# First MoE, last two token blocks: the up products in Strassen's form, with weight sums made in blocks 0 and 1

## The chip, the core and the metric

The kernel runs on one core of a Trainium2 chip. The metric is the device time of one execution in microseconds. The engines are named as in the profile: PE is TensorE's matmul (PEld its weight load), DVE is VectorE, ACT is ScalarE, POOL is GpSimd, SP is SyncE, which here issues the DMAs. PSUM is the memory of eight banks that PE writes to, SBUF the working memory.

## What is computed

Three stages follow one another, all in float32:

```python
# attention, B, H, S, D = 4, 8, 576, 64: causal softmax beside a linear memory
local = softmax(mask(q @ k.T / sqrt(D))) @ v
mem   = (phi(q) @ M_prev) / (phi(q) @ z_prev + 1e-6)
x = (g * mem + (1 - g) * local)            # -> (2304, 512)
# first MoE, d_ff = 2048
h = x @ w_in
y = (h * sigmoid(h)) @ w_out
# second MoE, d_ff = 1536
a = y @ w_gate
out = (a * sigmoid(a) * (y @ w_val)) @ w_out2
```

## The kernel before

A product of two float32 matrices is made from three matmuls: every operand is split into a rounded high part and the rest (hi and lo), and hi.hi, lo.hi and hi.lo are added up in PSUM. A matmul takes 128 x 128 weights and up to 512 columns. ACT makes hi by a cast, DVE or POOL makes lo by a subtraction.

The tokens of the first MoE stand in six blocks: two of batch 0 (256 and 320 tokens) and four of 432 tokens, named t0 to t3. d_ff is cut in 16 tiles j of 128, four tiles to a slice. A *segment* is one block with one slice: four h groups (`s1`, tile j of the up side: 3 x 4 = 12 matmuls into a bank of the pool `ps_m`), then four y groups (512 outputs in four parts e, 12 matmuls each). After an h group comes silu: tanh on ACT (th), a combination on DVE (th again), a cast on ACT (gh), the rest on POOL (gl). `segs` lists the segments in order: blocks of batch 0, then t0 with its four slices, t1 with its four, and then t2 and t3 together, slice by slice. The last 64 groups are those of t2 and t3, called the tail here.

Attention runs beside this: `units` are its steps (batch, pair of heads), cut into slots; a list of goals (`gds`, `gam`) says by which share of the first MoE's work a slot is due. A unit ends with U, the sum of its two parts in PSUM, which `put_x` splits into x (hi on ACT, lo on DVE). x of t2 and t3 is complete with the last unit only.

A third stream is the preparation of the second MoE's weights, `prep_w2`: load a raw tile (`load64`, after a small copy on POOL from the newest gl but one), decode it (L731 on ACT, L732 and L733 on DVE), make sums for Strassen's form on POOL (S), split the parts (cast wo on ACT, subtraction wo on POOL) and store them (`post`, `flush`) to DRAM. The scratch wo has `pw` = 3 buffers. A step of it is taken for 0.55 of the groups from group 50 on; when attention's slots are all placed, `open_w2` closes attention's pools, opens those of the second MoE, takes 0.6 steps a group, and also makes the second MoE's first inputs (`y_prep(0)`: casts of 768 columns on ACT and subtractions of 768 columns on DVE).

The program is written down in this order and then reordered by a scheduler within every engine; `high_priority` lets a part stand earlier. On the chip each engine takes its instructions in the order that came out, and waits on semaphores.

Of the kernel before, what the change touches and what calls it, by code (L numbers as in the profile page):

```python
# [17 lines left out]
P = 128  # L18
# [32 lines left out]
    gds=[0.75, 0.3, 1.25, 0.15, 0.3, 0.5, 1.5, 1.5],  # L51
# [4 lines left out]
    rate=0.55,  # L56
    late=0.6,
    ring=16,
    y0=36,
# [34 lines left out]
def kernel(  # L94
# [251 lines left out]
    def unit(u):  # L346
# [247 lines left out]
        def AV():  # L594
# [33 lines left out]
            for sup, U in Us.items():  # L628
                put_x(b, p, sup, U, E)

# [79 lines left out]
    def load64(w, j, part, after=None):  # L710

        raw = cur["raw"].tile([P, 512, 2], I32, tag="raw8", name="raw8", bufs=CFG["raw8"])
# [12 lines left out]
    def decode(raw, t=None):  # L725
        hi, lo = raw[:, :, 1], raw[:, :, 0]
        u = hi.bitcast(F32)
        if t is None:
            t = cur["raw"].tile([P, 512], F32, tag="raw", name="raw", bufs=CFG["raw"])
# [11 lines left out]
    def raw_w1(*key):  # L741
        if key in seen:
            return None
        if key[0] == 0:
            return load64(w1_in, key[1], 0)
        raw = cur["raw"].tile([P, 512, 2], I32, tag="raw8", name="raw8", bufs=CFG["raw8"])
# [9 lines left out]
    def split_w1(t, key):  # L756
        if key in seen:
            w = wp.tile([P, 2, 512], F32, tag="w", name="w")
            nc.sync.dma_start(out=w, in_=seen[key])
            return r_(w[:, 0]), r_(w[:, 1])  # L760
# [3 lines left out]
        return r_(w[:, 0]), r_(w[:, 1])  # L764

# [49 lines left out]
    for blks in [(0,), (1,), tuple(range(2, NB1))]:  # L815
        for s in [order[-1][1]] + [x for x in range(NSL) if x != order[-1][1]]:
            order += [(("t", i), s) for i in blks]
    segs = []
    for n, (key, s) in enumerate(order):
# [3 lines left out]
            last_use=n + 1 < len(order) and order[n + 1][1] != s,  # L823
        ))

    yps = {}

    def new_yp(key):
# [9 lines left out]
        return t[:, x0:x0 + KD * n].rearrange("p (k n) -> p k n", k=KD)  # L838

    def moe1():  # L840
# [12 lines left out]
        def s1(n, ji):  # L853
# [5 lines left out]
            if ji == 0 and sg["last_use"]:  # L859
                nk = SLICES[segs[n + 1]["s"]]  # L860
                prep1.add([(0, c) for c in nk])
                fresh[0] += len(nk)
            wh, wl = prep1.need((0, j))
# [10 lines left out]
            th = mt.tile([P, TM], F32, tag="th", name="th", bufs=CFG["th"])  # L874
            gh = mg.tile([P, TM], F32R, tag="gh", name="gh")
            gl = mg.tile([P, TM], F32R, tag="gl", name="gl")
            nc.scalar.activation(out=th[:, :nt], in_=ps[:, :nt], func=ACTF.Tanh, scale=0.5 / WS)  # L877
            nc.vector.scalar_tensor_tensor(th[:, :nt], th[:, :nt], 1.0, ps[:, :nt], ALU.add, ALU.mult)  # L878
            cp(CFG["gh" if n >= CFG["n0"] else "gh0"], gh[:, :nt], th[:, :nt])
            tt(CFG["gl" if n >= CFG["n0"] else "gl0"]).tensor_sub(gl[:, :nt], th[:, :nt], f(gh[:, :nt]))  # L880
            gs[n][j] = (gh, gl)
            gate.append(gl[:, 0:1])
# [9 lines left out]
        turn = [0]  # L892

        def bank(name):

            if "g" not in ph2:
                return ps_m.tile([P, 512], F32, tag="m", name=name)
            turn[0] += 1
            i = turn[0] % 7
            if i < 3:  # L900
                return ps_m.tile([P, 512], F32, tag="m", name=name)
            return sum_bank("bd"[i % 2], name)

        LA = CFG["la"]
        for n, sg in enumerate(segs):
# [9 lines left out]
            if n + 1 == len(segs):  # L915
                stream(-1)
            if n + 1 < len(segs) and LA:
                yield from get_x(n + 1)
                for ji in range(LA):
                    yield from s1(n + 1, ji)  # L920
            for e in range(KD):
                ps = bank("y")
                m, last = 0, 3 * len(SLICES[s]) - 1
                for wi, gi in ((0, 0), (1, 0), (0, 1)):
                    for ji, j in enumerate(SLICES[s]):
                        w, g = prep1.need((1, s, e))[wi], gs[n][j][gi]
                        c = slice(P * ji, P * ji + P)
                        nc.tensor.matmul(ps[:, :nt], w[:, c], g[:, :nt], start=(m == 0), stop=(m == last))  # L928
                        m += 1
                if sg["first"]:  # L930
                    nc.scalar.mul(yp[:, e, :nt], ps[:, :nt], 0.5 / WS**2)
                else:
                    nc.vector.scalar_tensor_tensor(
                        yp[:, e, :nt], ps[:, :nt], 0.5 / WS**2, yp[:, e, :nt], ALU.mult, ALU.add
                    )
                if sg["last"]:
                    nc.sync.dma_start(
                        out=yd[P * e:P * e + P, t0:t0 + nt], in_=yp[:, e, :nt]
                    )
                if sg["last_use"]:  # L940
# [4 lines left out]
                    prep1.add([(1, segs[n + 1]["s"], e)])  # L945
# [3 lines left out]


# [19 lines left out]
    def prep_w2():  # L970
        todo = [(j, part) for j in range(F2) for part in range(2)] + [(j, 2) for j in range(F2)]
        raws, post = [], []
# [5 lines left out]

        def flush():
            for d, t in post:  # L980
                nc.sync.dma_start(out=d, in_=t)
            post.clear()
# [9 lines left out]
        def halves(src, n, *dst):  # L992
            w = cur["pw"].tile([P, 4, 256], F32, tag="o", name="wo", bufs=CFG["pw"])
            hi, lo = hl(w, n)
            cp(CFG["whi2"], hi, src)
            tt(CFG["wlo2"]).tensor_sub(lo, src, f(hi))
            if len(dst) == 1:
                post.append((dst[0], w[:, 0:2 * n]))
            else:
                for x, d in enumerate(dst):  # L1000
                    post.append((d, w[:, 2 * x:2 * x + 2]))

# [5 lines left out]
        e = tt(CFG["sS"])  # L1008
        fetch(2)
        for j in range(F2):  # L1010
# [4 lines left out]
            S = cur["pw"].tile([P, 4, 256], F32, tag="S", name="S2", bufs=1)  # L1015
            e.tensor_add(S[:, 0], c[:, 0], c[:, 1])
# [7 lines left out]
            yield  # L1024
            halves(S[:, 2:4], 2, wd2[j][2])
            halves(c[:, 1:2], 1, wd2[j][3])
            yield paused()
        for q in range(NJ2):
# [12 lines left out]
            S = cur["pw"].tile([P, 4, 256], F32, tag="S", name="S2", bufs=1)  # L1041
            e.tensor_sub(S[:, 0], a[:, 1], a[:, 0])
# [6 lines left out]
            yield  # L1049
            halves(S[:, 0:2], 2, to("T1"), to("T2"))  # L1050
# [10 lines left out]
    def y_prep(i):  # L1061
# [9 lines left out]
        def put(nm, src):  # L1071
            y = ph2["yq"].tile([P, 2, 2, HT], F32, tag="y" + nm, name="y" + nm, bufs=1)
# [22 lines left out]
    def open_w2():  # L1095
        yield from drain()
# [3 lines left out]
        ph2["yq"] = ctx.enter_context(tc.tile_pool(name="yq", bufs=1, side="right"))  # L1100
        ph2["yst"] = ctx.enter_context(tc.tile_pool(name="yst", bufs=1, side="right"))
        ph2["xp"] = ExitStack()
        cur["raw"] = ph2["xp"].enter_context(tc.tile_pool(name="rawp2", bufs=1, side="right"))
        cur["pw"] = ph2["xp"].enter_context(tc.tile_pool(name="pw2", bufs=1, side="right"))
        n, y = 0, y_prep(0)
        while left() > 0:
            n += 1
            if int(n * CFG["late"]) > int((n - 1) * CFG["late"]):
                next(ph2["prep"], None)
            if left() <= CFG["y0"] and n % 4 == 1:  # L1110
                next(y, None)
            yield
        for _ in y:
            pass
        for _ in ph2["prep"]:
            pass

    def drain():

        ph2["hold"] = True  # L1120
        for x in ph2["prep"]:
            yield
            if x == "empty":
                break
            yield
        del ph2["hold"]

    def left():

        return sum(2 * NW for _ in segs) - ph2["n"]  # L1130
# [3 lines left out]
    def open_2():  # L1134
        ph2["xp"].close()
# [265 lines left out]
    if True:  # L1401
# [7 lines left out]

        def turn_of(rate):  # L1410
            return int((n_g + 1) * rate) > int(n_g * rate)

        goals, cost, prevc = [], 0, 0
        for sg in segs:
# [4 lines left out]
            prevc = seg_cost(sg)  # L1419
        cost, n_goal = 0, len(goals)  # L1420
        for kind, val in items:
            if kind == "need":
                while slot < val:
# [4 lines left out]
                    slot += 1  # L1428
            else:
# [12 lines left out]
                if slot < NSLOT:  # L1442
                    if "prep" in ph2 and n_g >= CFG["n_prep"] and turn_of(CFG["rate"]):
                        next(ph2["prep"], None)
                else:
                    if "late" not in ph2:
                        ph2["late"] = open_w2()
                    next(ph2["late"], None)
                n_g += 1
                ph2["n"] = n_g  # L1450
# [50 lines left out]
```

## Time and profile before

| | |
|---|---|
| median of 3 runs | 1061.36 us (1060.56 to 1063.29) |
| the profiled execution | 1062.63 us, span 1060.5 us |
| mean granted TensorE clock | 0.992 |
| PE busy | 1035.6 us, 98% of the span |
| DVE, ACT, POOL busy | 637.0, 539.6, 394.6 us |
| end of attention's last U on PE | 501.27 us |
| last matmul of the first MoE | 656.95 us |

The span is measured from the first to the last instruction; the rest of the time lies around it. A busy share is an average over stages. A wait is put down to the engine that released it last.

### The profile page before, as it was taken

How to read it: one execution, taken by the hardware profiler on the slowest of the kernel's cores; microseconds unless marked ns; L12 is line 12 of the kernel's file. 1: busy time of each engine (PE TensorE's matmuls, PEld its weight loads, DVE VectorE, ACT ScalarE, POOL GpSimd, SP SyncE). 2: the span in 40 equal slices, each digit the busy share in tenths (PEclk: the TensorE clock that was granted, in tenths of full speed). 3: DMA queues.
4: the chain of work that ended last, by engine and by line, in shares of the span. 5: the costliest groups of instructions: out<-in, count | busy, mean ns of one | idle time of the engine just before them, and what ended most of it. 6: DMA issues, size and time to landing. Idle time of an engine off the chain costs nothing.

```text
span 1060.5 us, 18824 instructions
## 1 busy us (share of the span) xinstructions
PE 1035.6 (98%) x6622; PEld 954.9 (90%) x6622; DVE 637.0 (60%) x1521; ACT 539.6 (51%) x1259; POOL 394.6 (37%) x461
## 2 busy tenths in 40 slices
PE   7799999999999999999999999999999999999998
PEld 5677988888888899888889999999999999999998
DVE  6796767876555644764254333566845669356573
ACT  6684877866656655664454331333613336133351
POOL 4784654678646556661578751000000000000000
PEclk9899999999999999999999999999999999999999
DMA  8995866468978569852478976777977778877784
GB/s 204 317 301 154 255 225 194 120 231 271 307 248 269 174 226 342 255 191 81 159 244 317 321 250 223 251 256 249 340 261 265 248 250 286 256 265 246 251 287 145
DMA packets 168670, 258.16 MB, mean 243 GB/s; under 512 B 76800, under 2 KB 113152, under 8 KB 168576
## 3 DMA queue, kind: packets, MB, share of 16 engines
q1 hardware_dynamic: 167488, 256.70, 73.1%
q8 instruction: 53, 0.87, 0.3%
q10 hardware_dynamic: 1088, 0.26, 0.1%
q14 instruction: 41, 0.34, 0.1%
HBM read 197.67 MB, written 59.24 MB: 242 GB/s over the span
## 4 chain that ended last, share of the span: by engine, by line
PE 78%; DMA 6%; DVE 4%; POOL 4%; ACT 4%; issue 3%; SPq 1%; POOLq 0%; DVEq 0%; ACTq 0%
PE y L928 15%; PE h L870 13%; PE oac L1205 11%; PE gb L1205 11%; PE po L1312 9%; PE pb L1312 4%; PE gd L1205 4%; PE U L619 3%; PE pst L367 3%; PE pss L434 3%; DMA raw<-in_moe_w_gate_dram 2%; DMA raw<-in_moe_w_val_dram 2%; DVE raw L733 1%; PE pss L509 1%; POOL gl L880 1%
## 5 line engine op out<-in xcount | busy, mean ns | idle before, releaser
L870 PE MATMUL h<-x,w 128*128 128x432 f32 (+2 forms) x1152 | 228.3, 348 | 5.9 <-ACT w L214 3.3
L870 PEld LDWEIGHTS h<-x,w 128*128 128x128 f32 x1152 | 197.8, 191 | 18.3 <-ACT w L214 3.5
L928 PE MATMUL y<-gh,w 128*128 128x432 f32 (+2 forms) x768 | 166.2, 348 | 4.2 <-ACT gh L214 2.3
L928 PEld LDWEIGHTS y<-gh,w 128*128 128x128 f32 x768 | 132.0, 190 | 15.3 <-issue 3.8
L880 POOL TENSOR_TENSOR gl<-th,gh 128x432 fp32r<-128x432 f32 (+2 forms) x96 | 104.7, 1093 | 81.7 <-ACT gh L214 64.9
L1205 PE MATMUL gb<-yT,w 128*128 128x384 f32 x648 | 124.8, 336 | 0.0
L1205 PEld LDWEIGHTS gb<-yT,w 128*128 128x128 f32 x648 | 113.1, 188 | 0.0
L878 DVE SCALAR_TENSOR_TENSOR th<-th,h 128x432 f32<-128x432 f32 (+2 forms) x96 | 52.6, 550 | 79.0 <-ACT th L877 78.9
L523 POOL TENSOR_TENSOR s<-s,r 128x128 f32<-128x128 f32 (+4 forms) x96 | 68.4, 739 | 73.4 <-DVE r L540 20.5
L1312 PE MATMUL po<-w,ph 128*128 128x256 f32 x516 | 93.8, 283 | 0.0
L928 PE MATMUL y<-gl,w 128*128 128x432 f32 (+2 forms) x384 | 88.4, 343 | 0.0
L490 ACT ACTIVATE s<-s,mn 128x128 f32<-128x128 f32 (+3 forms) x128 | 71.0, 557 | 21.4 <-DVE mn L486 19.9
L1205 PE MATMUL oac<-yB,w 128*128 128x384 f32 x432 | 81.3, 336 | 0.0
L1312 PEld LDWEIGHTS po<-w,ph 128*128 128x128 f32 x516 | 81.2, 191 | 0.0
L1277 ACT CAST ph<-r 128x384 fp32r<-128x384 f32 x108 | 51.1, 512 | 55.9 <-DVE r L1231 35.6
L1205 PEld LDWEIGHTS oac<-yB,w 128*128 128x128 f32 x432 | 75.4, 188 | 0.0
L732 DVE TENSOR_SCALAR raw<-raw 128x512 int32<-128x512 int32 x68 | 38.3, 564 | 58.1 <-ACT raw L731 57.8
L214 ACT CAST gh<-th 128x432 fp32r<-128x432 f32 (+2 forms) x96 | 49.0, 513 | 47.0 <-DVE th L878 33.8
L1312 PE MATMUL po<-w,pl 128*128 128x256 f32 x258 | 73.0, 283 | 0.0
L731 ACT ACTIVATE raw<-raw 128x512 f32<-128x512 f32 x68 | 45.6, 671 | 50.0 <-DMA raw<-in_moe_w_gate_dram 19.9
L928 PEld LDWEIGHTS y<-gl,w 128*128 128x128 f32 x384 | 67.6, 190 | 2.9 <-issue 0.5
L1278 DVE TENSOR_TENSOR pl<-r,ph 128x384 fp32r<-128x384 f32 x108 | 55.8, 553 | 17.8 <-ACT ph L1277 17.1
(161 smaller groups left out, 1993.2 us busy)
## 6 DMA issues: line engine op xcount, KB each, us to landing
w<-wg SPq DMA_DIRECT2D x108, 512.0 KB, 4.7
w<-wd SPq DMA_DIRECT2D x80, 512.0 KB, 5.8
wg<-wo SPq DMA_DIRECT2D x36, 512.0 KB, 3.7
w<-woT SPq DMA_DIRECT2D x36, 512.0 KB, 4.7
wd<-w SPq DMA_DIRECT2D x32, 512.0 KB, 4.2
raw<-in_moe_w_out_dram SPq DMA_DIRECT2D x28, 512.0 KB, 5.7
w<-woB SPq DMA_DIRECT2D x27, 512.0 KB, 4.3
w<-wg SPq DMA_DIRECT2D x36, 256.0 KB, 4.8
```

The lines of the kernel that those rows point to most:

```text
L214: nc.scalar.copy(out, in_)
L490: nc.scalar.activation(out=a, in_=a, func=ACTF.Exp, scale=-1.0, bias=mn, accum_out=o["sm", sup][:, col:col + 1])
L523: nc.gpsimd.tensor_mul(a, a, r.to_broadcast([P, w]))
L731: nc.scalar.activation(out=t, in_=u, func=ACTF.Prelu, scale=2.0**-111, alpha=-(2.0**32))
L870: nc.tensor.matmul(ps[:, :nt], w[:, kk, :], x[:, kk, :nt], start=(m == 0), stop=(m == 3 * KD - 1))
L878: nc.vector.scalar_tensor_tensor(th[:, :nt], th[:, :nt], 1.0, ps[:, :nt], ALU.add, ALU.mult)
L880: tt(CFG["gl" if n >= CFG["n0"] else "gl0"]).tensor_sub(gl[:, :nt], th[:, :nt], f(gh[:, :nt]))
L928: nc.tensor.matmul(ps[:, :nt], w[:, c], g[:, :nt], start=(m == 0), stop=(m == last))
L1205: nc.tensor.matmul(dst, w[wi][:, P * kk:P * kk + P], y[ny][:, yi, kk], start=(start and m == 0), stop=(stop and m == 5), skip_group_check= ...
L1277: nc.scalar.copy(ph, src)
L1278: nc.vector.tensor_sub(pl, src, f(ph))
L1312: nc.tensor.matmul(dst, a[:, c], x, start=(begin and m == 0 and own_bank), stop=(end and m == 2), skip_group_check=True,)
```

## The change

The up side of t2 and t3 is no longer made by tile and block. For each of eight pairs of tiles (ja, jc), the 2 x 2 product (two halves of d_model, K0 and K1; two blocks) is made by seven products instead of eight, each of 6 matmuls of 432 columns: `TP` names the weight sides, `TX` the token sides. The weight sums S1 to S4 are made in `combine`, for half of the pairs in t0's segments and for half in t1's, from the weights that lie in SBUF there, and stored to DRAM. The token sums T1 to T4 are made in `first_x` (T1, in the place of x's K0 half of t3) and `tail_x`. The products of a pair go into the banks ha, hb, hc, hd; ACT copies ha into hb and hc into he, DVE adds into hd and he, and four silus follow (`out_of`). The y groups of a slice stand among the products of the next one (`plan`). Preparation starts at group 40 with rates by group, is paused at group 112, and in the tail waits 14 groups and then goes on at 0.45; `y_prep(0)` comes after it.

```diff
-    gds=[0.75, 0.3, 1.25, 0.15, 0.3, 0.5, 1.5, 1.5],
+    gds=[0.75, 0.3, 1.25, 0.15, 1.8],
-    rate=0.55,
-    late=0.6,
+    rate=((40, 0.4), (50, 0.6), (64, 0.75), (96, 0.65)),
+    hold=112,
+    late=0.45,
+    late0=14,
+    urgent=300,
...
-    for blks in [(0,), (1,), tuple(range(2, NB1))]:
+    for blks in [(0,), (1,)]:
...
+    def combine(ja, jc):
+        flush()
+        t = cur["pw"].tile([P, 4, 256], F32, tag="o", name="wo", bufs=CFG["pw"])
+        a, c = (t.rearrange("p a b -> p (a b)")[:, 512 * x:512 * x + 512] for x in range(2))
+        for t, j in ((a, ja), (c, jc)):
+            hi, lo = kept_w[j]
+            nc.vector.tensor_add(t, f(hi), f(lo))
+        S = cur["pw"].tile([P, 4, 256], F32, tag="o", name="wo", bufs=CFG["pw"])
+        nc.vector.tensor_add(S[:, 0], c[:, 0:256], c[:, 256:512])
+        nc.vector.tensor_sub(S[:, 1], S[:, 0], a[:, 0:256])
+        nc.vector.tensor_sub(S[:, 2], a[:, 0:256], c[:, 0:256])
+        nc.vector.tensor_sub(S[:, 3], a[:, 256:512], S[:, 1])
+        for x in range(2):
+            d = seen["S", ja, x] = dram.tile([P, 4, 256], F32, name=f"wsum{ja}_{x}")
+            halves(S[:, 2 * x:2 * x + 2], 2, d)
...
+    TP = ("A11", "S1", "S2", "A12", "S3", "S4", "A22")
+    TX = ("B11", "T1", "T2", "B21", "T3", "B22", "T4")
...
+            if n == 0:
+                ys_ = [("z", e) for e in range(KD)]
+                plan = "p y y p y p p y p p p"
+            else:
+                plan = "p p y p p y p p y p y" if ys_ else "p p p p p p p"
...
+            if p == 0:
+                o["a"] = ph2["ta"].tile([P, 512], F32, tag="a", name="ha")[:, :TB]
+                product(o["a"], it, True)
+                if n > 0:
+                    o["b"] = seeded("b", n)
+                    with urgent():
+                        nc.scalar.copy(o["b"], o["a"])
+            elif p == 1:
...
+                c = sum_bank("d", "hc")[:, :TB]
+                product(c, it, True)
+                o["e"] = ph2["tt"].tile([P, TB], F32, tag="e", name="he", bufs=2)
+                with urgent():
+                    nc.scalar.copy(o["e"], c)
+            elif p == 2:
+                product(o["b"], it, False)
+                o["d"] = seeded("d", n)
+                with urgent():
+                    nc.vector.tensor_add(o["d"], o["b"], o["e"])
+            elif p == 3:
+                product(o["a"], it, False)
+                out_of(n, 0, 0, o["a"])
+            elif p == 4:
+                product(o["b"], it, False)
+                with urgent():
+                    nc.vector.tensor_add(o["e"], o["b"], o["e"])
+                out_of(n, 1, 1, o["e"])
+            elif p == 5:
+                product(o["d"], it, False)
+                out_of(n, 0, 1, o["d"])
+            else:
+                product(o["b"], it, False)
+                out_of(n, 1, 0, o["b"])
...
+    def tail_x():
+        x0, x1 = (xs["t", 2 + h] for h in range(NH))
...
+        whole(a, x1, K0)
+        whole(c, x0, K0)
+        nc.vector.tensor_sub(b, whole(d, x1, K1), a)
+        tx = [ph2["tt"].tile([P, 2, 2, TB], F32R, name="x" + nm) for nm in ("T2", "T3", "T4")]
+        split_x("T2", b, tx[0][:, 0], tx[0][:, 1])
+        nc.vector.tensor_sub(a, b, c)
+        split_x("T3", a, tx[1][:, 0], tx[1][:, 1])
+        nc.vector.tensor_sub(d, whole(d, x0, K1), b)
+        split_x("T4", d, tx[2][:, 0], tx[2][:, 1])
```

What the scheduler makes of it is seen at three places. On PE, where attention ends: U is its last product, h and y are groups of the first MoE. Before:

```order
L619 MATMUL U<-tb,v_t_102 64x320 x6
L619 MATMUL U<-ta,v_t_102 64x128
L870 MATMUL h<-x,w 128x432 x66
L928 MATMUL y<-gh,w 128x432 x8
L928 MATMUL y<-gl,w 128x432 x3
```

In the changed program, where a row with one hb or hd is a matmul that only opens a bank, xT_6939 and xT_6940 are T2 and T3, and x is B11, T1 or B21:

```order
L621 MATMUL U<-ta,v_t_102 64x128 x2
L1074 MATMUL ha<-x,w 128x432 x6
L1084 MATMUL hb<-x,w 128x432
L1074 MATMUL hc<-x,w 128x432 x6
L1084 MATMUL hd<-x,w 128x432
L1084 MATMUL hb<-x,w 128x432
L1074 MATMUL ha<-x,w 128x432 x6
L1074 MATMUL hb<-xT_6939,w 128x432 x4
L1074 MATMUL hc<-x,w 128x432 x6
L1074 MATMUL hb<-xT_6939,w 128x432 x2
L1074 MATMUL ha<-x,w 128x432 x6
L1074 MATMUL hb<-xT_6940,w 128x432 x6
```

Where 66 matmuls of h stood, 33 of the products stand ahead of the third ha row, which is the second pair's first product. On DVE at the same place, x<-U is the low part of attention's last x. Before:

```order
L342 TENSOR_TENSOR x<-U,x 128x320
L342 TENSOR_TENSOR x<-U,x 128x144
L342 TENSOR_TENSOR x<-U,x 128x112
L1080 TENSOR_TENSOR yt<-ytop 128x768
L878 SCALAR_TENSOR_TENSOR th<-th,h 128x432
```

In the changed program, where wo and S_6934 are scratch for the token sums and L1168 makes their low parts:

```order
L344 TENSOR_TENSOR x<-U,x 128x320
L1159 TENSOR_TENSOR wo<-x 128x864 x2
L344 TENSOR_TENSOR x<-U,x 128x144
L344 TENSOR_TENSOR x<-U,x 128x112
L1159 TENSOR_TENSOR S_6934<-x 128x864
L1188 TENSOR_TENSOR wo<-S_6934,wo 128x864
L1191 TENSOR_TENSOR wo<-wo 128x864
L1159 TENSOR_TENSOR S_6934<-x 128x864
L1168 TENSOR_TENSOR xT_6939<-wo,xT_6939 128x864
L1193 TENSOR_TENSOR S_6934<-S_6934,wo 128x864
L1168 TENSOR_TENSOR xT_6940<-wo,xT_6940 128x864
L861 SCALAR_TENSOR_TENSOR th<-th,ha 128x432
```

Two sums of 864 columns stand between the pieces of x<-U, and seven more operations of that size ahead of the first silu. The third place is DVE in the last unit of attention, where the last weight sum (L892 to L897) stands among attention's masked minimum (L488, L512):

```order
L892 TENSOR_TENSOR wo<-w 128x512 x2
L344 TENSOR_TENSOR x<-U,x 128x320
L344 TENSOR_TENSOR x<-U,x 128x144
L344 TENSOR_TENSOR x<-U,x 128x112
L488 ISA s_6462,mn_6388<-pss,mask 128x512
L488 ISA mn_6388 128x1
L894 TENSOR_TENSOR wo<-wo 128x256
L896 TENSOR_TENSOR wo<-wo 128x256
L488 ISA s_6465,mn_6388<-pss,mask 128x512
L488 ISA mn_6388 128x1
```

The rows L892, L894 and L896 are new there; the first of L892 and L894 wait for stores of earlier contents of wo.

## Rows read from the trace of the kernel before

**Rows 1.** The page: busy time, share and instructions of each engine.

```profile
PE 1035.6 (98%) x6622; PEld 954.9 (90%) x6622; DVE 637.0 (60%) x1521; ACT 539.6 (51%) x1259; POOL 394.6 (37%) x461
```

**Rows 2.** By stage: length, PE, PEld, DVE, ACT, POOL busy, PE clock, DMA.

```profile
225.00:501.30 276.30, 271.29 (x1709) 236.16 (x1703) 164.36 (x459) 172.41 (x421) 169.31 (x204) 0.99 0.71 236
501.30:545.00 43.70, 40.01 (x193) 37.37 (x194) 20.38 (x32) 21.95 (x42) 22.18 (x23) 0.96 0.49 167
545.00:656.80 111.80, 111.80 (x571) 106.62 (x570) 40.79 (x65) 41.98 (x80) 72.67 (x78) 1.00 0.80 276
```

**Rows 3.** Chain that ended last, in the tail: start, length, what.

```profile
567.35 9.43 PE h L870 x48
576.78 9.39 PE y L928 x48
```

**Rows 4.** Timeline of PE from attention's end: start, length, [idle before, releaser].

```profile
500.89 0.38 PE L619 MATMUL U<-ta,v_t 128*64 128x128 f32 x2
501.21 6.20 PE L870 MATMUL h<-x,w 128*128 128x432 f32 x30
508.82 7.33 PE L870 MATMUL h<-x,w 128*128 128x432 f32 x36 [1.42 <-DVE th L878]
...
538.84 1.05 PE L928 MATMUL y<-gh,w 128*128 128x432 f32 x4 [2.27 <-ACT gh L214]
539.73 4.00 PE L870 MATMUL h<-x,w 128*128 128x432 f32 x12
...
656.00 0.95 PE L928 MATMUL y<-gl,w 128*128 128x432 f32 x4
```

**Rows 5.** The stretch after the 2.27 us wait, columns of rows 2.

```profile
539.70:543.50 3.80, 3.80 (x14) 3.54 (x13) 2.23 (x4) 1.71 (x4) 3.74 (x4) 0.58 0.01 2
```

**Rows 6.** DVE after attention's end: its timeline, and a group by shape.

```profile
501.63 0.71 DVE L342 TENSOR_TENSOR x<-U,x 128x320 fp32r<-128x320 f32 x2 [3.27 <-ACT x L214]
502.66 0.28 DVE L342 TENSOR_TENSOR x<-U,x 128x112 fp32r<-128x112 f32 x1 [0.32 <-ACT x L214]
507.29 0.96 DVE L1080 TENSOR_TENSOR yt<-ytop 128x768 f32<-128x768 f32 x1 [4.36 <-DMA ytop<-yd]
508.16 0.60 DVE L878 SCALAR_TENSOR_TENSOR th<-th,h 128x432 f32<-128x432 f32 x1
...
L1074 DVE TENSOR_TENSOR yT<-yt,yT 128x768 fp32r<-128x768 f32 x2 | 1.9, 946 | 0.0
```

**Rows 7.** ACT's casts of 768 columns: count, busy, mean ns, idle before.

```profile
L1073 ACT CAST yT<-yt 128x768 fp32r<-128x768 f32 x2 | 1.6, 824 | 0.0
```

**Rows 8.** Groups by line over the span, columns of rows 7.

```profile
L996 POOL TENSOR_TENSOR wo<-S,wo 128x512 fp32r<-128x512 f32 x36 | 48.3, 1345 | 9.0 <-ACT wo L214 9.0
L214 ACT CAST wo<-S 128x512 fp32r<-128x512 f32 x36 | 22.2, 620 | 26.7 <-POOL S L1017 12.5 <-DMA woT<-wo 4.5 <-POOL S L1019 3.0
L342 DVE TENSOR_TENSOR x<-U,x 128x256 fp32r<-128x256 f32 (+6 forms) x44 | 15.6, 370 | 19.2 <-ACT x L214 18.9
L1247 DVE TENSOR_TENSOR gd<-gb,e 128x384 f32<-128x384 f32 x36 | 20.4, 566 | 4.3 <-PE gd L1216 3.8 <-PE gb L1205 0.3
L996 POOL TENSOR_TENSOR wo<-raw,wo 128x512 fp32r<-128x512 f32 (+1 forms) x36 | 40.4, 1121 | 27.2 <-ACT wo L214 27.2
```

**Rows 9.** ACT's waits for DMAs, 495 to 655 us: total, times, longest.

```profile
ACT raw L731 <- DMA raw<-in_moe_w_out_dram: 15.0, 11, 4.0
ACT wo L214 <- DMA woT<-wo: 7.4, 3, 4.5
ACT wo L214 <- DMA woB<-wo: 6.0, 4, 2.5
```

**Rows 10.** PE's timeline at the start of the second MoE.

```profile
658.78 1.32 PE L1205 MATMUL oac<-yT,w 128*128 128x384 f32 x6 [0.60 <-ACT gb L1239]
```

**Rows 11.** DMA issues: count, size, median us from issue to landing.

```profile
w<-wg SPq DMA_DIRECT2D x108, 512.0 KB, 4.7
w<-wd SPq DMA_DIRECT2D x80, 512.0 KB, 5.8
```

More of the change, by code (lines that the diff above doesn't have):

```diff
@@ L741, in raw_w1 @@
     def raw_w1(*key):
-        if key in seen:
+        if key in seen or key[0] == "c":
             return None
@@ L873, in s1 @@
                     m += 1
[L874 to L882, printed above, removed]
+            gs[n][j] = silu(ps[:, :nt], nt, mg, n < CFG["n0"])
+            if sg["key"] in (("t", 0), ("t", 1)) and ji == 1 + 2 * sg["key"][1]:
+                combine(j - 1, j)
             if sg["last_use"]:
@@ L890, in s1, with sums @@
             yield ("g", 12 * nt)
-        turn = [0]
         def bank(name):
[L896 to L902, printed above, removed]
+            return ps_m.tile([P, 512], F32, tag="m", name=name)
+        def sums(ps, key, s, e, g, first, last):
+            t0, nt, yp = key["t0"], key["nt"], yps[key["key"]]
+            m, end = 0, 3 * len(SLICES[s]) - 1
+            for wi, gi in ((0, 0), (1, 0), (0, 1)):
+                for ji, j in enumerate(SLICES[s]):
+                    w = prep1.need((1, s, e))[wi]
+                    c = slice(P * ji, P * ji + P)
+                    nc.tensor.matmul(ps[:, :nt], w[:, c], g[j][gi][:, :nt], start=(m == 0), stop=(m == end))
+                    m += 1
+            if first:
+                nc.scalar.mul(yp[:, e, :nt], ps[:, :nt], 0.5 / WS**2)
+            else:
+                nc.vector.scalar_tensor_tensor(
+                    yp[:, e, :nt], ps[:, :nt], 0.5 / WS**2, yp[:, e, :nt], ALU.mult, ALU.add
+                )
+            if last:
+                nc.sync.dma_start(out=yd[P * e:P * e + P, t0:t0 + nt], in_=yp[:, e, :nt])
         LA = CFG["la"]
@@ L920, in moe1 @@
                     yield from s1(n + 1, ji)
+            if n + 1 == len(segs):
+                yield from tail(lambda e: sums(bank("y"), sg, s, e, gs[n], sg["first"], sg["last"]), sums, bank)
+                return
             for e in range(KD):
[L922 to L939, printed above, removed]
+                sums(bank("y"), sg, s, e, gs[n], sg["first"], sg["last"])
                 if sg["last_use"]:
@@ L1093, in y_prep, with open_tail @@
         yield
-    def open_w2():
-        yield from drain()
+    def open_tail():
+        ph2["hold"] = True
+        while "empty" not in ph2:
+            prep_step()
+        del ph2["hold"]
+        flush()
         cur["x"].close()
@@ new lines, in open_tail, with prep_step, late @@
+        tail_x()
+        ph2["late"] = late()
+    def prep_step():
+        if "empty" not in ph2 and next(ph2["prep"], None) == "empty":
+            ph2["empty"] = True
+    def late():
+        n = 0
+        for _ in range(CFG["late0"]):
+            yield
+        for _ in ph2["prep"]:
+            while True:
+                n += 1
+                yield
+                if int(n * CFG["late"]) > int((n - 1) * CFG["late"]):
+                    break
+        ph2["xp"].close()
+        ph2["yst"] = ctx.enter_context(tc.tile_pool(name="yst", bufs=1, side="right"))
+        ph2["yq1"] = ctx.enter_context(tc.tile_pool(name="yq1", bufs=1, side="right"))
+        y = y_prep(0)
+        for _ in range(3):
+            next(y)
+            yield
+            yield
+        while "yq" not in ph2:
@@ L1112, in open_w2, with close_tail @@
             yield
         for _ in y:
[L1114 to L1121, printed above, removed]
-            yield
[L1123 to L1130, printed above, removed]
+            yield
+    def close_tail():
+        ph2["ttx"].close()
+        while "yst" not in ph2:
+            next(ph2["late"])
+        ph2["yq"] = ctx.enter_context(tc.tile_pool(name="yq", bufs=1, side="right"))
+        stream(-1)
```

248 lines of the change are left out of this document (198 added, 50 removed).

## The prediction

> **What bounds the kernel now.** I read the engines' totals first, then a table by stage, then TensorE's own timeline around the edited stage, and last what the helper engines wait for. TensorE (PE) is busy 98% of the span, the next engine 60% [rows 1]: time can only come from fewer matmul columns or from smaller holes in PE. The table by stage [rows 2] shows where holes are. From 225 to 501.3 us, where attention runs beside first-MoE blocks, PE lacks 276.3 - 271.3 = 5.0 us. From 501.3 to 545 us, the opening of the last two blocks, it lacks 3.7 us and its clock is 0.96. From 545 to 656.8 us it lacks nothing.
>
> A matmul of 432 columns costs 9.43 / 48 and 9.39 / 48, so 0.196 us, in the undisturbed runs of that stage [rows 3]. In the timeline [rows 4] attention's last U matmul ends at 500.89 + 0.38 = 501.27 us and the last y matmul at 656.95 us: 155.7 us for 64 groups of 12, which are 768 x 0.196 = 150.5 us of work. The missing 5.2 us are three things: a wait of 1.42 us on VectorE's th, one of 2.27 us on ScalarE's gh, and then twelve matmuls in 4.00 us instead of 12 x 0.196 + 0.17 = 2.5, because the granted clock was 0.58 (mostly the 1.2 GHz level) right after that wait [rows 5].
>
> **The change, part by part.**
>
> *Columns.* In the instruction order, the h matmuls go from 1152 to 768, and ha, hb, hc, hd are 96 + 146 + 48 + 49 = 339 new ones, all 128x432; everything else on PE keeps its count. So 45 matmuls fewer (8 pairs x 6, less 3 that only open a bank): 45 x 0.196 = **-8.8 us**. TensorE: Matmul & The Clock Gate of the Trainium skill (Back-to-back issue gap) gives N / 2.4 + 2.5 ns, 182.5 ns at 432 columns, against the measured 196; by it this term would be an estimated -8.2, and the measurement decides.
>
> *The old holes of this stage.* The 1.42 us wait came from y's preparation: VectorE stood 4.36 us before L1080 for a load of yd, and th behind it came late [rows 6]. The 2.27 us wait was gh behind casts and decodes on ScalarE, and the slow clock followed it. After the change, y's preparation is spread over the end of the tail and these queues stand otherwise, so I take all of it away: **-5.2 us**. What may come in their place is counted in the next terms.
>
> *The new opening.* Before, PE goes from U straight into h, with no wait [rows 4]. After, all of ha, hb, hc and hd lie in the banks that attention frees, and by its waits the first ha needs the last x<-U on VectorE. Before, that x<-U ended 502.66 + 0.28 = 502.94, 1.7 us after PE's U [rows 6]. Now two sums of 864 columns stand ahead of its last two pieces, and the first of them waits for the last U too. A 768-column subtraction takes 0.946 us [rows 6], so 864 columns take 1.06: PE stands 1.7 + 2 x 1.06 = 3.8 us. Then VectorE has seven more such operations in its order before th<-ha (0.60 us) frees bank ha for the second pair: 3.8 + 7 x 1.06 + 0.6 = 11.8 us. PE has 33 matmuls ahead of that point, 6.5 us, so it loses 5.3 us up to there, whether it waits at that bank or spends 1.5 us in a slow clock after the first wait (as in rows 5); the second swallows the first. T2's cast (864 columns, 0.93 us by [rows 7]) is ready at 3.8 + 2 x 1.06 + 0.9 = 6.9, before PE's 3.8 + 21 x 0.196 = 7.9. Then T4's low part (1.06) and the add into hd (0.57 [rows 8]) end at 13.4 against PE's 13.0: 0.4 more. **+5.7 us**; between 4.7 (the sums in 0.95) and 7 (the slow clock added in full).
>
> *Work put into blocks 0 and 1.* Eight weight sums: on VectorE, by 1.23 ns a column, 16 adds of 512 (0.63) and 32 of 256 (0.37 [rows 8]), 22 us; on ScalarE 16 casts at 0.62, 10 us; on GpSimd 16 subtractions at 1.345, 21.5 us [rows 8]; T1 adds 4 x 1.06 on VectorE. The order also shows 3 of 13 decodes and 7 of 27 casts moved from the tail to before the last U: some 8 us of GpSimd, 6 of ScalarE, 4 of VectorE. From 225 us that makes VectorE some 194 of 276 us, ScalarE 188, GpSimd 199, from 164, 172 and 169 [rows 2]: none becomes the bound. What can reach PE is waiting in a queue: each weight sum has two VectorE instructions that wait until a scratch buffer's store has landed. Of such waits ScalarE's casts show 13.4 us [rows 9] over 72 casts, 0.19 each; 16 x 0.19 = 3 us; and of VectorE's 4.36 us on a load 1.42 reached PE [rows 4, 6], a third. **+1.0 us**, the nearest rows; nothing if the sums fall into idle time, up to the first rival's price if they do not. In favour, the filler matmuls between attention's last units are more even: in the order 157, 100, 96, 61 where 226, 84, 71, 39 stood; that could give back half of this stage's 5.0 us at best.
>
> *The rest of the tail.* ScalarE now copies ha into hb and hc into he on PE's path: at most 0.6 us were lost where the second MoE does the same [rows 10]. Cover is the next product, 6 x 0.196 = 1.2 us, and from the third pair on a y group of 2.4 besides. In the same queue 10 decodes and 20 casts remain, before which ScalarE stood 28.4 us in the old tail [rows 9], unseen by PE then. I take **+1.0 us**, between 0 (rows 10's stage goes on without holes) and the second rival's price.
>
> *At nothing.* 16 stores and 16 loads of sums: loads land in 4.7 to 5.8 us [rows 11], and the buffers are asked for 7 us or more ahead of use (33 matmuls at the start); if a load is late there, its lateness is a hole. Preparation's end and y's last four pieces: 8 groups of 2.4 us stand behind them.
>
> *Sum.* -8.8 - 5.2 + 5.7 + 1.0 + 1.0 = **-6.3 us**. The profiled execution took 1062.63 us (span 1060.5, 2.1 around it), so 1056.3; it lies 1.3 above the median of the three runs, 1061.36, which gives **1055.1 us**.
>
> **The rivals.** A measurement of this kernel can tell about 0.3%, 3.2 us, from no change.
>
> *Weight sums block attention (slower).* Place: the two adds of each sum in VectorE's queue, with attention's masked minimum and silu's th behind them, and PE in order behind these. If every sum meets one store wait as long as the longest seen, 4.5 us [rows 9], that is 36 us, a third of it 12 us in PE instead of 1.0: +4.7, so 1066 us. It decides the sign from 7.3 us of holes, 22 us of VectorE waits, 1.4 us for each of the 16. For it: such waits are there on ScalarE. Against: 0.19 us each so far. The Trainium skill's TensorE: Matmul & The Clock Gate (Architectural detail) says that ScalarE and VectorE are strict first-in first-out; the trace agrees, with the 1.42 us hole above.
>
> *ScalarE's waits for loads reach PE (no change).* Place: decodes and casts of the preparation ahead of hb<-ha and he<-hc. The old tail's 28.4 us scale with 10/13 and 20/27 to about 21; if a quarter passes the cover, 5 us in place of 1.0: 1059.1. For it: the cover is 1.2 us in two pairs, and waits reach 4.5. Against: 3.5 us of cover with a y group, in the other six.
>
> *The opening is longer (no change).* If the clock stays low for two stretches and loads are late, the opening costs 9 instead of 5.7, so 1058.4.
>
> That fewer columns are not what runs is ruled out by the count.
>
> **How the numbers follow.** Forecast 0.61; sums block attention 0.15; the other two together 0.24, half of it within 0.3% of before. Faster needs less than 1058.2. So faster 0.63 (forecast and a few of the middle cases), same 0.21, slower 0.16. Low end: -8.8 - 5.2 + 4.7, and 2.5 of the attention stage's holes gone: 1049 to 1050. High end: between the middle rivals and the first, 1064, which leaves out about one in ten.
>
> **What would show it.** Right: 45 fewer 432-column matmuls; a hole of about 3.8 us before the first ha, named x<-U on VectorE; a wait of about 1.5 us at bank ha or a low clock before it; few holes from there to the second MoE; the stage from last U to last y about 148 us. Wrong: holes over 7 us between 225 us and the last U (VectorE behind stores), waits of PE on hb<-ha behind ScalarE's decodes, or a hole at the start of the second MoE.

## The result, and the profile after

The changed kernel takes 1074.32 us (median of 4 runs, 1072.86 to 1075.79), the kernel before, run beside it, 1062.23: ratio 1.0115, 95% interval 1.0092 to 1.0138. It is slower by 12 us (1.2%), clear of the noise, where 1055.1 was forecast and 1064 was the end of the range. The profiled execution took 1073.26 us, span 1071.1, 10.6 more than the span before. In its timeline attention's last U ends at 513.55 us and the last y matmul at 662.14, which cuts the difference in three:

| stretch, us | before | changed | difference | forecast |
|---|---|---|---|---|
| start to the end of the last U | 501.3 | 513.55 | +12.3 | +1.0 |
| last U to last y (the tail) | 155.7 | 148.6 | -7.1 | -8.8 - 5.2 + 5.7 + 1.0 = -7.3 |
| last y to the span's end | 403.5 | 409.0 | +5.4 | 0 |

The tail came out near the forecast; the loss lies on both sides of it. The page's row of busy times, in the place of [rows 1]:

```profile
PE 1034.2 (97%) x6577; PEld 949.5 (89%) x6577; DVE 725.1 (68%) x1619; ACT 558.4 (52%) x1295; POOL 407.7 (38%) x457
```

The 45 matmuls are gone, and VectorE has 88 us more. The table by stage, columns as in [rows 2]: attention, the opening of the tail, the tail from 545 us on, the start of the second MoE:

```profile
225.00:513.60 288.60, 276.19 (x1719) 237.41 (x1715) 220.20 (x523) 186.89 (x449) 208.56 (x232) 0.99 0.83 282
513.60:545.00 31.40, 28.21 (x136) 26.85 (x137) 20.31 (x29) 15.58 (x30) 9.68 (x11) 0.95 0.55 186
545.00:662.20 117.20, 115.89 (x589) 110.18 (x587) 71.28 (x107) 52.96 (x101) 55.69 (x51) 1.00 0.85 298
650.00:675.00 25.00, 22.02 (x101) 20.64 (x100) 6.47 (x10) 1.90 (x4) 0.00 (x0) 0.86 0.69 226
```

Beside attention PE lacks 12.4 us, 5.0 before [rows 2], and VectorE is busy 220 us where 194 was forecast. The waits of PE in that stretch (total, times, longest), the first four:

```profile
PE y L968 <- DVE th L861: 4.1, 5, 1.4
PE psk L369 <- DVE mr L457: 1.6, 2, 1.2
PE pss L436 <- DVE tb L218: 1.4, 2, 1.0
PE h L941 <- DVE th L861: 1.3, 1, 1.3
```

Most are on VectorE, none on a weight sum itself: silu's th, the linear memory's mr and the copy tb come late in the same queue. PE's timeline at the two ends of the tail:

```profile
512.73 0.82 PE L621 MATMUL U<-ta,v_t 128*64 128x256 f32 x8
516.79 1.64 PE L1074 MATMUL ha<-x,w 128*128 128x432 f32 x6 [3.24 <-DVE x L344]
...
661.18 0.96 PE L968 MATMUL y<-gl,w 128*128 128x432 f32 x4
664.57 2.29 PE L1453 MATMUL oac<-yB,w 128*128 128x384 f32 x6 [2.42 <-DVE x L973]
```

The first wait is the forecast one (3.8 forecast, 3.24 measured). Behind it the granted clock is 0.66 from 516.79 to 520 us and 0.70 from there to 522, and PE reaches the third ha row at 524.91 without another wait: 33 matmuls took 8.1 us instead of 6.5, so the lower clock cost 1.6, where the prediction had 1.5 us of low clock or of waiting at bank ha. The second wait was forecast as nothing, and behind it six matmuls of 384 columns take 2.29 us where [rows 10] have 1.32: the granted clock is 0.50 there (the 1.2 GHz level, 664.6 to 667 us), 0.86 on average in the last row by stage. VectorE at the second place, and the chain of waits that leads there:

```profile
652.16 1.19 DVE L973 SCALAR_TENSOR_TENSOR yp<-y,yp 128x432 f32<-128x432 f32 x2 [2.33 <-PE y L968]
...
659.82 0.61 DVE L973 SCALAR_TENSOR_TENSOR yp<-y,yp 128x432 f32<-128x432 f32 x1 [1.74 <-PE y L968]
663.04 0.96 DVE L1312 TENSOR_TENSOR yt<-ytop 128x768 f32<-128x768 f32 x1 [2.62 <-DMA ytop<-yd]
663.91 0.60 DVE L973 SCALAR_TENSOR_TENSOR x<-y,x 128x432 f32<-128x432 f32 x1
```

```profile
653.62 4.39 DMA yd<-yp
658.07 4.87 DMA ytop<-yd
```

The add into yt opens the inputs of the *second* block of the second MoE, which nothing needs before the first block is done. It stands in VectorE's order ahead of the last y sum and waits for t2's first two parts of y, whose sums end at 653.35 and which then go to DRAM and back in 4.39 + 4.87 = 9.3 us. Before, t2's four last y groups stood ahead of t3's four; now the two blocks are mixed, and t2's come later. The second MoE's first product needs what the last y sum releases.

### The profile page after: what moved, and what is told of

Same layout as the page of the kernel before. It is cut to its first block, busy times and chain, and to the rows that moved or that the text cites. A ratio compares the mean times of both kernels' runs of the same rounds, so it can differ in the third digit from the quotient of the medians.

```text
span 1071.1 us, 18998 instructions
## 1 busy us (share of the span) xinstructions
PE 1034.2 (97%) x6577; PEld 949.5 (89%) x6577; DVE 725.1 (68%) x1619; ACT 558.4 (52%) x1295; POOL 407.7 (38%) x457
## 4 chain that ended last, share of the span: by engine, by line
PE 70%; DVE 10%; DMA 8%; ACT 4%; POOL 4%; issue 3%; SPq 1%; DVEq 0%; POOLq 0%; ACTq 0%
PE y L968 12%; PE oac L1453 11%; PE gb L1453 11%; PE po L1560 9%; PE h L941 5%; PE pb L1560 4%; PE gd L1453 4%; PE hb L1074 3%; DMA wg<-wo 3%; PE pss L436 2%; PE U L621 2%; PE pst L369 2%; PE ha L1074 2%; DVE raw L737 2%; POOL wo L878 1%
## 5 line engine op out<-in xcount | busy, mean ns | idle before, releaser
L941 PE MATMUL h<-x,w 128*128 128x432 f32 (+2 forms) x768 | 150.4, 340 | 5.8 <-ACT w L216 2.9
L941 PEld LDWEIGHTS h<-x,w 128*128 128x128 f32 x768 | 124.8, 191 | 15.1 <-ACT w L216 3.2
L736 DVE TENSOR_SCALAR raw<-raw 128x512 int32<-128x512 int32 x68 | 44.1, 650 | 35.7 <-ACT raw L735 35.6
L488 DVE CUSTOM_DVE_ANT_0 s<-pss,mask 128x128 f32<-128x128 f32 (+3 forms) x128 | 58.4, 484 | 13.6 <-PE pss L436 13.3
L1473 DVE SCALAR_TENSOR_TENSOR sg<-sg,gd 128x384 f32<-128x384 f32 x36 | 20.0, 554 | 65.6 <-ACT sg L1472 65.6
```

The lines of the kernel that those rows point to most:

```text
L488: nc.vector.tensor_tensor_reduce(out=a, in0=at[i](hh), in1=mask[:, 512 - w:512], op0=ALU.add, op1=ALU.min, scale=1.0, scalar=3.0e38, accum ...
L941: nc.tensor.matmul(ps[:, :nt], w[:, kk, :], x[:, kk, :nt], start=(m == 0), stop=(m == 3 * KD - 1))
```

## The experiments

Beside every group of runs the kernel before was run again (1061.5 to 1062.4 us), and ratios are to it.

**1. No sums.** `combine` stores what it has instead of sums; the six adds on VectorE, the two casts, the two subtractions and the four scratch buffers of each pair go:

```diff
-        t = cur["pw"].tile([P, 4, 256], F32, tag="o", name="wo", bufs=CFG["pw"])
...
-            halves(S[:, 2 * x:2 * x + 2], 2, d)
+            post.append((d[:, 0:2].rearrange("p a b -> p (a b)"), f(hi)))
+            post.append((d[:, 2:4].rearrange("p a b -> p (a b)"), f(lo)))
```

> The changed kernel with the weight sums not computed: the raw high and low parts of the two weights are stored in their place, so the stores and loads stay and the arithmetic of the sums is left out (the output is not the reference's). Theory A (the sums' VectorE, ScalarE and GpSimd work holds up attention's queues): the end of the last U comes back from 513.5 to about 503 us, and the time from 1074.3 to 1063 to 1066 us. Theory B (the pace of the preparation and the new goals do it): the last U stays at 510 us or later and the time at 1070 us or more.

1055.07 us, ratio 0.9931 (0.9910 to 0.9953). The sums' arithmetic, with the scratch buffers that it takes, costs 19 us between the medians, 16.5 between the profiled spans. (That the forecast's number comes out is chance: the opening is shorter here and the second MoE starts later than forecast.) Its timeline has the last U at 493.64 us with 39 matmuls of the first MoE more behind it (7.6 us), so that the end of U compares as 501.3 with 513.55: 12.3 us. The rest, 3.9 us of the 16.5, is the tail, where those y matmuls cover the wait for x<-U. Beside attention PE lacks 2.9 us, 12.4 with the sums; the row by stage, and PE's longest wait:

```profile
225.00:493.70 268.70, 265.77 (x1689) 231.19 (x1686) 181.18 (x475) 178.23 (x437) 181.02 (x216) 0.99 0.86 290
PE h L932 <- DVE th L861: 2.1, 1, 2.1
```

The wait at the second MoE is still there:

```profile
648.49 1.31 PE L1444 MATMUL oac<-yB,w 128*128 128x384 f32 x6 [2.56 <-DVE x L964]
```

**2. The preparation's pace of before.** `rate=((50, 0.55),)`, `late=0.6`.

> The changed kernel with the preparation paced as before (from group 50 at 0.55, 0.6 in the tail). Theory A: the sums stay, so the last U stays at 510 us or later and the time at 1071 to 1077 us. Theory B (pace): the last U at about 503 to 506 us, the time 1064 to 1067 us.

1077.29 us, 1.0141 (1.0120 to 1.0162). Neither theory as written: the last U is at 503.73 us with 27 more matmuls behind it (5.3 us), so 4.5 us are won there; but preparation then ends late, and the second MoE waits for its inputs:

```profile
667.24 2.29 PE L1453 MATMUL oac<-yB,w 128*128 128x384 f32 x6 [13.43 <-DMA ybot<-yd]
```

**3. The kernel before, with the sums added and not used.**

> The kernel before with the eight weight sums added in the same places of blocks t0 and t1, split and stored, and not read by anything. Theory A: they alone cost most of the 13 us: 1070 to 1074 us. Theory B: under 1065 us.

1072.64 us, 1.0106 (1.0071 to 1.0140): the sums alone, with their stores, cost 10.3 us, nothing else of the change being there. Its last U ends at 514.11 us.

**4. The add into yt behind the last y sum**, an edge of order on VectorE that moves one row, for the second block only:

```diff
+            with tc.issue_after(last_y[0].ins):
                 nc.vector.tensor_sub(t, t1, t0)
```

> The changed kernel with one VectorE instruction (the add into yt that opens the inputs of the second block of the second MoE) put behind the last y sum instead of ahead of it. If its wait for the load of ytop is what held the second MoE's first product: the 2.4 us wait of oac on x goes, with the low clock behind it, 4 to 5 us in all, so 1069.5 to 1070.5 us. If another wait (banks, buffers, the loads themselves) stands right behind it: 1072 to 1075 us.

1070.90 us, 1.0083 (1.0063 to 1.0103): 3.4 us less. PE's timeline there, with the clock full again:

```profile
663.08 0.96 PE L968 MATMUL y<-gl,w 128*128 128x432 f32 x4
664.74 1.31 PE L1457 MATMUL oac<-yB,w 128*128 128x384 f32 x6 [0.70 <-DVE x L973]
```

From last y to the last matmul it takes 401.5 us, 406.0 in the changed kernel, 400.6 in the kernel before.

**5 and 6. Half of the sums' work each:** the adds without the split, then the split (cast, subtraction) without the adds.

> The changed kernel with VectorE's adds of the weight sums kept, and their split left out (no ScalarE cast, no GpSimd subtraction; the sums are stored unsplit, as many bytes; the output is not the reference's). With no sums at all the time was 1055.1, with all of them 1074.3 us. Theory V (VectorE's adds in front of silu and attention cost the time): 1068 to 1074 us. Theory Q (the split does: casts that stand in ScalarE's queue before a scratch buffer is stored, and 16 more subtractions on GpSimd): 1055 to 1060 us. If the two add up: 1061 to 1067 us.

> The changed kernel with VectorE's adds left out: the cast, the subtraction and the store of each half are made on the weights' high parts instead (the output is not the reference's). Theory V: 1055 to 1060 us. Theory Q: 1068 to 1074 us. If the two add up: 1061 to 1067 us.

Adds only: 1064.37 us, 1.0016 (0.9999 to 1.0033), 9.3 above none. Splits only: 1060.55 us, 0.9983 (0.9963 to 1.0002), 5.5 above none. The two make 14.8 of the 19.2; 4.4 us more come when both are there. Neither theory's range is met by both runs, and the second lies just under the range for adding up: no single engine is to blame. Beside attention PE lacks 10.0 us with the adds and 5.5 with the splits, 2.9 with neither.

**7. Three scratch buffers for a combination instead of four.**

> The changed kernel with the same sums made in fewer buffers: the first weight gets a buffer of its own, the second is added up in place, so a combination takes three buffers of the ring of three instead of four. If waiting for stores of the ring is the cost: 1064 to 1069 us. If it is the work itself: 1071 to 1076 us.

1076.46 us, 1.0125 (1.0089 to 1.0161). Fewer buffers of the ring give nothing back. That does not clear waits for stores: ScalarE's casts still wait 11.0 us for them beside attention, 13.1 in the changed kernel.

**8. The same spread over groups**, the preparation standing still meanwhile:

```diff
+        work.extend([second, third, fourth, flush])
...
+                if work:
+                    work.pop(0)()
```

> As the one with fewer buffers, and the six adds and two splits of a combination written one or two to a group instead of all at once, the preparation standing still meanwhile. If bursts in front of silu and attention are the cost: 1062 to 1068 us. If the busy time of VectorE and GpSimd as a whole is: 1070 to 1076 us.

1084.02 us, 1.0182 (1.0139 to 1.0226), worse than both said. The preparation held back has to be made up later; in its profile PE's longest wait (4.6 us on th, at 503 us) lies in the last 50 us before the end of attention at 518.9, another of 2.9 us on gl at 404. That the one makes the other was only read off, not tried apart.

**9. Sums of six pairs in the tail**, from weights in SBUF into the weight buffers:

```diff
+        if key[0] == "S" and key not in seen:
+            return tail_sums(*key[1:])
```

> The changed kernel with the sums of the first two pairs made in blocks t0 and t1 as before, and those of the other six pairs made in the tail itself, from the weights that lie there, straight into the weight buffers (no store and no load of sums; the second weight of the pair is loaded instead). In the tail GpSimd is busy 65 of 148 us and VectorE 90, beside attention 209 and 220 of 288 us. Theory A (the sums cost time because they meet attention on busy engines): six eighths of the 19 us between all sums and none come back, so about 1060 us. Rival (the sums cost as much in the tail, where silu and the products wait for VectorE as well): 1068 us or more.

1076.40 us, 1.0156 (1.0131 to 1.0182): the rival. The last U comes at 502.38 us with 21 more matmuls behind it (4.1), so 7.1 are won there; the tail, less those 4.1, takes 157.1 instead of 148.6. Its waits of PE from 502 to 664 us:

```profile
PE hb L1105 <- ACT hb L1138: 5.5, 2, 4.3
PE hb L1105 <- DVE he L1160: 1.5, 1, 1.5
PE y L999 <- DVE x L1004: 1.1, 1, 1.1
PE ha L1105 <- DVE th L892: 1.0, 1, 1.0
```

Rows of busy time had said that the tail has room (VectorE 90 of 148 us). The longest waits stand behind ScalarE's copies of ha into hb.

**10 to 12. The opening, all three, and pace.** Number 10 has number 4 and the first two token sums behind x<-U; 11 has 9 and 10; 12 has 11 with the earlier pace and a faster tail.

```diff
+        with tc.issue_after(last_x[0].ins):
             whole(a, x1, K0)
             whole(c, x0, K0)
```

> The changed kernel with two orders on VectorE changed: the add into yt behind the last y sum (measured above: 1070.9 us), and the first two token sums of the tail behind the last piece of x<-U instead of ahead of it. If the 3.2 us that PE stands before the first ha hang on those two sums: the wait falls to about 1.2 us and the time to about 1069 us. If T2 to T4 and the first silu are late then instead: 1071 us.

> The sums of six pairs in the tail, the add into yt behind the last y sum, and the token sums behind x<-U, all three. Theory A: 1060 less 3.4 less 2, about 1054.5 us, faster than the kernel before. Rival (work in the tail shows up as waits of PE on VectorE): 1062 us or more.

> All three as above, with the preparation paced as before beside attention (from group 50 at 0.55) and resumed earlier and faster in the tail (after 4 groups, 0.65). With the earlier pace alone the last U came 10 us sooner and the second MoE started 13 us late. If less preparation beside attention still helps when the sums are gone from there, and the tail takes it in time: 1050 to 1053 us. If the preparation then ends late: 1058 us or more, with PE waiting for ybot at the second MoE's first product.

Number 10: 1074.36 us, 1.0124 (1.0106 to 1.0142), 3.5 worse than 4. The wait for x<-U falls from 3.2 to 1.4 us as meant, and one on the copy of ha comes in its place:

```profile
PE hb L1076 <- ACT hb L1109: 3.2, 2, 2.3
PE ha L1076 <- DVE x L346: 1.4, 1, 1.4
```

Number 11: 1066.44 us, 1.0059 (1.0038 to 1.0079), 10 better than 9, still slower than before: the second case of its expectation. Number 12: 1096.14 us, 1.0321 (1.0289 to 1.0352), its second case in time but not in place: PE waits on gh, he, hb and th all over the tail (6.2, 4.8, 3.4 and 4.1 us), not on ybot.

**13. Earlier pace, sums where they were, number 4's order.**

> The changed kernel, sums beside attention as they were, with the add into yt behind the last y sum, the preparation paced as before beside attention (from group 50 at 0.55), and resumed after 4 groups of the tail at 0.62 instead of 14 at 0.45. If preparation and sums share one loss beside attention, and the tail has room for preparation: last U at about 504 us, tail 150, second MoE 401.5, so about 1060.5 us. If the tail has no room: 1066 us or more, with waits of PE in the tail.

1073.42 us, 1.0121 (1.0093 to 1.0150), the second case. The last U comes at 504.64 us as forecast. Less its 27 more matmuls, the tail is 151.4 us instead of 148.6, and the second MoE waits 3.4 us for yT: preparation taken away from attention is missed elsewhere.

**14. The adds on GpSimd.** `nc.vector` in `combine` becomes `nc.gpsimd`.

> The changed kernel with the six adds of each combination on GpSimd instead of VectorE. If the cost sits in VectorE's queue (adds of two SBUF operands that take 0.42 us alone and about 1 us beside GpSimd, with silu and the masked minimum behind them): 1062 to 1068 us. If the sums cost in whichever queue silu passes through, since GpSimd makes gl: 1073 us or more.

1074.71 us, 1.0126 (1.0102 to 1.0150), as on VectorE.

**15. The kernel before with y's preparation later on VectorE.**

> The kernel before, without Strassen in the first MoE and without sums, with one order changed: VectorE's work on the second MoE's first inputs stands where it is written, in the second half of the tail, instead of right behind attention's last x. If the holes of 1.42 and 2.27 us in the old tail, with the low clock behind the second, hang on that order: 4 to 5 us less, 1057 us. If ScalarE's casts and decodes make them: 1060 to 1062 us.

1061.57 us, 0.9997 (0.9981 to 1.0012), the second case in time. The old holes of [rows 4] are gone, and as much stands in five new ones:

```profile
PE y L930 <- ACT gh L214: 3.6, 5, 1.2
```

**16 and 17. Do the losses add up, and go with the number of sums?** Number 16 is 1 and 4 together; 17 makes the sums of block t0 only.

> No weight sums (raw parts stored in their place, as in the first experiment; the output is not the reference's) and the add into yt behind the last y sum. If the sums and that wait are two separate losses: 1055.1 less 3.4, about 1051.7 us. If the last y sum's wait is hidden once the sums are gone: 1055 us.

> Weight sums of the four pairs made in block t0 only; for the four of block t1 raw parts are stored in their place (the output is not the reference's). If every sum costs the same: half way between 1055.1 and 1074.3, about 1064.7 us. If the first ones fall into idle time and only the sum of all is too much: 1060 us or less.

Number 16: 1051.27 us, 0.9900 (0.9882 to 0.9919), 3.8 below number 1: two separate losses. Number 17: 1062.82 us, 1.0008 (0.9996 to 1.0021), 7.8 above none for half of the sums, of 19.2 for all: already the first half costs nearly its share.

## Why the prediction was wrong

**What held.** Columns: 45 matmuls fewer. Six of them, it turns out, are ahead of the last U: 762 stood behind it, not 768, so 39 went from the tail (7.6 us, not 8.8) and the old holes were 6.3 us, not 5.2. That the two errors cancel in the tail's sum is luck. The opening: 3.24 us for 3.8, low clock 1.6 for 1.5, and 723 matmuls x 0.196 = 141.7 us against 148.6 leaves 6.9 for opening and rest, forecast 5.7 + 1.0. The rest of the tail shows one wait, 1.25 us on the y sum. The old holes went with the change, but experiment 15 shows that moving VectorE's rows alone only puts others in their place.

**The step that failed: work put into blocks 0 and 1, +1.0 us.** It cost 12.3 us up to the last U, and 16.5 to 19 with what followed in the opening (experiment 1); put into the kernel before, 10.3 (experiment 3). Two things were wrong in it. The smaller is a price. I took the adds of 512 columns from a subtraction of 768 (0.63), those of 256 from the mean of L342 (0.37, [rows 8]), which reads PSUM and mixes seven shapes, and got 22 us of VectorE. Measured, the changed kernel's groups of sums beside attention, with silu and a step of the decode for comparison:

```profile
L861 DVE SCALAR_TENSOR_TENSOR th<-th,h 128x432 f32<-128x432 f32 x32 | 18.9, 594 | 10.3 <-ACT th L860 10.3
L892 DVE TENSOR_TENSOR wo<-w 128x512 f32<-128x512 f32 x16 | 15.0, 975 | 2.2 <-DMA woB<-wo 2.2
L894 DVE TENSOR_TENSOR wo<-wo 128x256 f32<-128x256 f32 x8 | 5.5, 693 | 0.0
L896 DVE TENSOR_TENSOR wo<-wo 128x256 f32<-128x256 f32 x8 | 5.5, 686 | 0.0
L897 DVE TENSOR_TENSOR wo<-wo 128x256 f32<-128x256 f32 x8 | 5.0, 622 | 0.0
L895 DVE TENSOR_TENSOR wo<-wo 128x256 f32<-128x256 f32 x8 | 4.7, 591 | 0.0
L736 DVE TENSOR_SCALAR raw<-raw 128x512 int32<-128x512 int32 x25 | 18.2, 728 | 15.1 <-ACT raw L735 15.1
```

The sums are 35.7 us. With the lengths that they have beside an idle GpSimd (0.68 for 512 columns, 0.41 for 256) they would be 24.0. The decode got longer too. Its two steps L736 and L737 take 43.9 us for 50 instructions, where the kernel before had 29.8 for 43; the first of them there:

```profile
L732 DVE TENSOR_SCALAR raw<-raw 128x512 int32<-128x512 int32 x21 | 10.5, 501 | 31.2 <-ACT raw L731 31.1
```

Sums and decode are most of the way from the 194 us forecast to the 220 measured. An add of 256 columns takes 0.41 us in one place and 1.07 in another, and what differs is GpSimd at the same time. VectorE, and then GpSimd in the same stretch:

```profile
253.38 0.95 DVE L894 TENSOR_TENSOR wo<-wo 128x256 f32<-128x256 f32 x1
254.26 1.07 DVE L896 TENSOR_TENSOR wo<-wo 128x256 f32<-128x256 f32 x1
...
255.86 0.59 DVE L861 SCALAR_TENSOR_TENSOR th<-th,h 128x432 f32<-128x432 f32 x1
256.38 0.41 DVE L895 TENSOR_TENSOR wo<-wo 128x256 f32<-128x256 f32 x1
...
257.48 0.59 DVE L861 SCALAR_TENSOR_TENSOR th<-th,h 128x432 f32<-128x432 f32 x1
...
258.33 1.42 DVE L897 TENSOR_TENSOR wo<-wo 128x256 f32<-128x256 f32 x1
```

```profile
253.14 0.92 POOL L1248 TENSOR_TENSOR S<-raw,S 128x256 f32<-128x256 f32 x1
254.02 1.04 POOL L863 TENSOR_TENSOR gl<-th,gh 128x320 fp32r<-128x320 f32 x1
255.12 0.26 POOL L719 COPY raw<-gl 128x1 f32<-128x1 f32 x1
257.12 1.12 POOL L863 TENSOR_TENSOR gl<-th,gh 128x432 fp32r<-128x432 f32 x1 [1.74 <-ACT gh L216]
258.18 1.29 POOL L878 TENSOR_TENSOR wo<-wo 128x512 fp32r<-128x512 f32 x1
```

The add at 256.38, with GpSimd idle, takes 0.41; those at 253.38, 254.26 and 258.33 began after an instruction of GpSimd and end some 0.28 us behind its end (254.06, 255.06 and 259.47). The Trainium skill's page SBUF — State Buffer (SBUF: two separate sides) says why: an instruction of VectorE with two inputs in SBUF and one of GpSimd that reads SBUF take turns at a shared pair of ports, and the later waits for the whole of the other. The trace agrees, and th, with one operand in PSUM, keeps its length (0.59 at 257.48, within GpSimd's gl). I had not weighed that rule.

The larger error is the third that I took from one wait. I let waits alone, not work, reach PE, and let a third of 3 us pass. Experiments 5, 6, 14 and 9 show that the work reaches PE whichever of the three queues carries it: adds 9.3 us, splits 5.5, the adds on GpSimd as much as on VectorE, six pairs in the tail as much as beside attention, and experiment 17 that it does so from the first sums on. Two of the prediction's three signs of being wrong came: 12.4 us of holes between 225 us and the last U, though hardly from VectorE behind stores, and a hole at the start of the second MoE.

**The first rival** had the place and the sign, but not the mechanism; that its 12 us in PE meet the 12.3 is luck. Waits for stores on VectorE are 2.2 us in one (the row of L892 above), not 36. There are more of them on ScalarE, from 225 us to the last U:

```profile
ACT wo L216 <- DMA wg<-wo: 10.3, 6, 5.3
ACT wo L216 <- DMA wsum<-wo: 2.8, 4, 1.1
```

That is 13.1 us, 2.1 without sums. They do not set the size of the loss: with the adds alone ScalarE waits 13.5 us so and the cost is 9.3, with the splits alone 14.8 and 5.5, and PE lacks 10.0 us in the one and 5.5 in the other. What share they have in the loss no run shows, since none keeps the work and removes these waits.

**The second failed step: "preparation's end and y's last four pieces", at nothing.** The eight y groups cover them, but not the same preparation's next block, whose first add the scheduler sets among them: 3.4 us (experiment 4), 3.8 without sums (experiment 16). In the kernel before the same instruction for the first block had made the 1.42 us hole, and I took that away without asking what stands behind the one for the second block; that one stood at 645.67 us there, ahead of the last y groups, and made PE wait nowhere.

The sum as it should have been, against spans: -7.1 + 12.3 + 5.4 = +10.6.

**Open.** How the 12.3 us divide: against the run without sums, idle time of PE beside attention is 9.5 of them (12.4 and 2.9); the rest no experiment took apart. Longer pauses ahead of 225 us (14.1 us of idle time, 12.6 in the kernel before) are not of the sums: without sums they are 14.5, and the first add stands at 246.89 us. How much of the loss is the work itself, the longer instructions beside it or the waits for stores, is open too. And whether weight sums can be made where they cost less than the columns save: none of the variants here that make all sums beat the kernel before (best, number 11, ratio 1.0059), and numbers 1 and 16, which make none, say what would be left if the sums cost nothing: 1055 and 1051 us.

## What to carry to other kernels

Price work that is added beside a PE-bound stage by the queues it enters, not by their busy share: here 35.7 us on VectorE, and 9.6 and 20.8 on ScalarE and GpSimd, with VectorE at 76% the busiest of them, cost 16.5 to 19 us, about twice the 8.8 saved. Take an instruction's length from a row with operands in the same memory and the same neighbour engine at work. When a stall is taken away, look for the instruction that waited and name what stands behind it in its new place.

## What the runs showed of the hardware

Adds of two SBUF operands on VectorE: 0.41 us for 256 columns beside an idle GpSimd, 0.85 to 1.42 in the eleven that a longer instruction of GpSimd had begun before, each ending 0.28 to 0.29 us behind that one's end. Three that began first (at 359.14, 364.56 and 497.10) kept 0.41 to 0.42. silu's th, with one operand in PSUM, is unaffected: median 0.60 us in 19 within GpSimd's instructions, 0.59 in 10 with GpSimd idle. On GpSimd (number 14) the adds take 1.47 us for 512 columns and 0.73 for 256:

```profile
L892 POOL TENSOR_TENSOR wo<-w 128x512 f32<-128x512 f32 x16 | 23.3, 1473 | 0.4 <-DMA woB<-wo 0.4
L894 POOL TENSOR_TENSOR wo<-wo 128x256 f32<-128x256 f32 x8 | 5.8, 730 | 0.2
```

A wait of 2.42 us at the second MoE's start was followed by six matmuls in 2.29 us instead of 1.31, at a granted clock of 0.50; with the wait cut to 0.70 (number 4) the clock stayed at 1.00. In number 1 a wait of 2.56 us was followed by six in 1.31 and, from 650.53 us on, the next product's six in 2.29: there the clock fell later.
